# Queries, keys and values laid out ahead of the launch, instead of transposed on the chip, in attention with two dense layers

## The chip, the cores and the metric

One core of one Trainium2 chip. A time is the device time of one execution of the whole program in microseconds (us). Engines: TensorE (PE for matmuls, PEld for its weight loads), VectorE (DVE), ScalarE (ACT), GpSimd (POOL) and SyncE (SP), which only issues transfers. SPq and ACTq are the queues on which SP and ScalarE issue transfers.

## The reference

Attention with 4 batches, 8 heads, 576 positions and head dimension 64, and then two layers over 2304 tokens:

```python
scores = scale * np.matmul(q, k.transpose(0, 1, 3, 2))
cum = np.cumsum(np.maximum(s, 0.0), axis=-1)
bias = -(cum[:, :, :, None] - cum[:, :, None, :])
scores = np.where(causal, -1e9, scores + np.minimum(bias, 0.0))
attn = softmax(scores)                       # with 1e-9 added to the sum
x = (attn @ v).transpose(0, 2, 1, 3).reshape(2304, 512)
x = leaky_relu(x @ w_in, 0.01) @ w_out       # 512 -> 2048 -> 512
out = softplus(x @ w2_in) @ w2_out           # 512 -> 2048 -> 512
```

Everything is 32-bit. The matmuls of the layers run as three products of a high and a low part.

## The kernel before

The program has an attention stage and a main stage. The attention stage goes over 16 pairs of heads (`p`, from 0 to 15, four pairs to a batch). The 576 positions are four blocks of 128 and a tail of 64. Each pair is worked off in four units, in the order: block 3, the tails of both heads together, block 2, blocks 1 and 0. The loop at L454 is a pipeline by hand: step `n` = 4`p` + `i` issues the scores of unit `n`+1, masking, maxima (L316) and exponentials (L330) of unit `n`, the division (L341) of unit `n`−1, the transposes of the probabilities (L353, L358) of unit `n`−2, and the evacuation (L370, L372) of unit `n`−3. `pv` (L374) multiplies by the values at `i` = 0 and 2, for the pair before. All engines work in the order of the program; `later(n, fn)` and `tick()` put a piece of work some half-steps further on.

Scores need queries and keys with the head dimension on partitions: tiles `Q` (128 x 640) and `K` (128 x 576), where the two heads of a pair lie in partitions 0 to 63 and 64 to 127. The queries of the two tails stand in columns of their own, with zeros in the other head's partitions. The decay bias comes as two rows for each operand, `BQ` and `BK`, added by a second matmul into the same bank. All of these have two buffers, by the parity of `p`. The bias rows are made once (`decay`, L152), written to a scratch tensor `bb_d` and read back pair by pair (`rows`, L227); for pair 0 they are moved straight from the tile `bb`.

Queries and keys arrive in HBM as batch, head, position, dimension. `load` (L210) brings them into staging tiles `rawq`, `rawk` (one buffer each) and `rawl` (the tails of both), two transfers for each with rows of 256 bytes. `prep` (L241) transposes them on TensorE: four transposes for `q`, four for `k`, one for the tails, into the single PSUM bank "a", which `pv` uses as well. Half a step later ScalarE copies the queries into `Q` (L256), VectorE copies the keys (L258) and the three pieces of the tails (L260, L263). `prep` of pair `p`+1 happens at `i` = 0 (queries), 1 (keys) and 2 (tails); right behind it stands the load for pair `p`+2. At `i` = 0 the bias rows of pair `p`+1 follow on SP's queue. Values of pair `p`+1 are loaded at `i` = 3 by three transfers (L221 twice, L225).

Beside this runs a filler (`Fill`, L499). `step` loads and splits weights of the first layer at fixed steps up to 45, and `run` issues one filler unit of twelve matmuls for each step (L141 or L586), once the tokens of a whole batch are done and the weights are there. So the first pairs have no filler, and later ones one unit in every step; what is left is worked off at the end. After the attention stage, the main stage runs the remaining groups of both layers with an order of its own (the loop at L732).

Of the kernel before, what the change touches and what calls it, by code (L numbers as in the profile page):

```python
# [9 lines left out]
F32 = mybir.dt.float32  # L10
# [3 lines left out]
AF = mybir.ActivationFunctionType  # L14
# [3 lines left out]
P = 128  # L18
# [11 lines left out]
@with_exitstack  # L30
def attn_moe_moe(ctx, tc, q, k, v, s, w1i, w1o, w2i, w2o, out):
    nc = tc.nc
    B, H, S, D = q.shape
    NT, DM = out.shape
    DFF = w1i.shape[1]
    KD = DM // P
# [3 lines left out]
    NP = B * NPAIR  # L40
    NB = S // P
    TL = S - NB * P
# [5 lines left out]
    def pool(name, bufs=1, **kw):  # L48
        return tc.tile_pool(name=name, bufs=bufs, **kw)
# [14 lines left out]
    def later(n, fn, *args):  # L64
        todo.setdefault(clock[0] + n, []).append((fn, args))

    def tick():
        clock[0] += 1
        for fn, args in todo.pop(clock[0], ()):
            fn(*args)  # L70
# [5 lines left out]
    def move(dst, src, queue=nc.sync):  # L76
        queue.dma_start(dst.bitcast(F32), src.bitcast(F32))
# [74 lines left out]
    def decay(cp, first):  # L152

        BH = B * H
        c0 = cp.tile([BH, S], F32, tag="c0", name="c0")
        c1 = cp.tile([BH, S], F32, tag="c1", name="c1")
        bb = cp.tile([BH, 2, 2, S], F32R, tag="bb", name="bb")
        one = bb[:, 0, 0, :].bitcast(F32)
        nc.sync.dma_start(c0, s.rearrange("b h s -> (b h) s"))
        first()  # L160
        nc.vector.memset(one, 1.0)

        nc.vector.tensor_scalar(c0, c0, 0.0, 1.0 / scale, op0=ALU.max, op1=ALU.mult)
        nc.vector.tensor_tensor_scan(c1, one, c0, 0.0, op0=ALU.mult, op1=ALU.add)
        nc.scalar.activation(bb[:, 1, 0, :], c1, AF.Copy)
        nc.scalar.activation(bb[:, 0, 0, :], c1, AF.Copy, scale=-1.0)
        hi = bb[:, 1, 0, :].bitcast(F32)
        nc.vector.tensor_tensor(bb[:, 1, 1, :], c1, hi, op=ALU.subtract)
        nc.vector.tensor_tensor(bb[:, 0, 1, :], hi, c1, op=ALU.subtract)
        return bb  # L170


    def attention(att, ps, fills):
        ident = att.tile([P, P], F32, tag="ident", name="ident")
# [7 lines left out]
        Q, K = two("Q", [P, ZQ]), two("K", [P, S])  # L182
        BQ, BK = two("BQ", [P, ZQ], F32R), two("BK", [P, S], F32R)
        V = two("V", [P, NB + 1, 2, D])
        raw = {nm: att.tile([P, NB, 2, D], F32, tag="raw" + nm, name="raw" + nm) for nm in "qk"}
        raw["l"] = att.tile([P, 2, D], F32, tag="rawl", name="rawl")

        PA = att.tile([P, 2, NB, P + TL], F32, tag="PA", name="PA")
        PZ = att.tile([P, 2, TL], F32, tag="PZ", name="PZ")
# [1 line left out]
        def blank(i):  # L191
            bq, bk = BQ[i].bitcast(F32), BK[i].bitcast(F32)
            nc.gpsimd.memset(bq, 0.0)
            nc.gpsimd.memset(bk, 0.0)
            for j in range(2):
                for c in own[j]:
                    nc.gpsimd.memset(bq[j * D:j * D + 2, c], 1.0)
                nc.gpsimd.memset(bk[j * D + 32:j * D + 34], 1.0)
                nc.gpsimd.memset(Q[i][(1 - j) * D:(2 - j) * D, NB * P + j * TL:NB * P + (j + 1) * TL], 0.0)

        def zeros():
            for i in range(2):
                nc.gpsimd.memset(V[i][TL:, NB, :, :], 0.0)
            nc.gpsimd.memset(PZ[TL:], 0.0)

        def heads(p):
            b, hp = divmod(p, NPAIR)
            return b, slice(2 * hp, 2 * hp + 2)

        def load(p, nm):  # L210
            if p >= NP:
                return
            b, hs = heads(p)
            src = {"q": q, "k": k, "v": v}.get(nm)
            if nm == "l":
                for x, r in ((q, slice(0, TL)), (k, slice(TL, 2 * TL))):
                    nc.sync.dma_start(raw["l"][r], x[b, hs, NB * P:, :].rearrange("h p d -> p h d"))
                return
            t = V[p % 2] if nm == "v" else raw[nm]
            for j in range(2):  # L220
                nc.sync.dma_start(  # L221
                    t[:, :NB, j, :], src[b, hs.start + j, :NB * P, :].rearrange("(c p) d -> p c d", p=P)
                )
            if nm == "v":
                nc.sync.dma_start(t[:TL, NB, :, :], src[b, hs, NB * P:, :].rearrange("h p d -> p h d"))  # L225

        def rows(p, src, queue=(nc.sync, nc.sync)):  # L227

            if p < NP:
                b, hs = heads(p)  # L230
                for j in range(2):
                    h, r = b * H + hs.start + j, j * D
                    of = lambda e, c: src[h, e, :, c] if src is bb_d else src[h:h + 1, e, :, c]
                    n = 0
                    for c in own[j]:
                        m = n + c.stop - c.start
                        move(BQ[p % 2][r + 32:r + 34, c], of(0, slice(n, m)), queue[j])
                        n = m
                    move(BK[p % 2][r:r + 2], of(1, slice(0, S)), queue[j])

        def prep(p, nm):  # L241

            if p >= NP:
                return
            tag, bufs = ("a", 1) if p or nm == "q" else ("m", 1) if nm == "k" else ("t", 2)
            pm = ps.tile([P, 512], F32, tag=tag, name="pt_qk", bufs=bufs)
            if nm == "l":
                nc.tensor.transpose(pm[:, :P], raw[nm].rearrange("p h d -> p (h d)"), ident)
            else:
                for c in range(NB):  # L250
                    nc.tensor.transpose(pm[:, c * P:(c + 1) * P], raw[nm][:, c].rearrange("p h d -> p (h d)"), ident)  # L251

            def out():
                qt, kt = Q[p % 2], K[p % 2]
                if nm == "q" or nm == "k" and not p:
                    nc.scalar.activation((qt if nm == "q" else kt)[:, :NB * P], pm, AF.Copy)  # L256
                elif nm == "k":
                    nc.vector.tensor_copy(kt[:, :NB * P], pm)  # L258
                else:
                    nc.vector.tensor_copy(kt[:, NB * P:], pm[:, TL:2 * TL])  # L260
                    for j in range(2):
                        r = slice(j * D, (j + 1) * D)
                        nc.vector.tensor_copy(qt[r, NB * P + j * TL:NB * P + (j + 1) * TL], pm[r, :TL])  # L263

            later(1, out)


        class Unit:
# [152 lines left out]
                )  # L421

        def first():
            for nm in "qkl":
                load(0, nm)

        with pool("cum", side="right") as cp:
            bb = decay(cp, first)
            blank(0)
            for nm in "qkl":  # L430
                prep(0, nm)
                tick()
            tick()
            rows(0, bb, (nc.sync, nc.scalar))
            masks()
            zeros()
            blank(1)
            load(1, "q")
            load(0, "v")
            move(bb_d, bb)  # L440
            load(1, "k")
            load(1, "l")
        fill = fills()
        order = [[NB - 1], [], [NB - 2], [1, 0]]
        units = [(p, ts) for p in range(NP) for ts in order]
# [8 lines left out]
        for n in range(len(units) + 3):  # L454
            p, i = divmod(n, len(order))
            u0, u1, u2, u3 = (live.get(n - d) for d in range(4))
            start(n + 1)
            if u0:
                u0.maxima(0)
                u0.exps(0)  # L460
            if u1:
                u1.divisors()
                u1.norm(0)
            if u2:
                u2.transpose(0)
            if u3:
                u3.evacuate(1)
            if i == 0:
                prep(p + 1, "q")
                load(p + 2, "q")  # L470
                rows(p + 1, bb_d)
            elif i == 2:
                prep(p + 1, "l")
                load(p + 2, "l")
            tick()
            if n == len(units):
                fill.free = [("m", 1), ("s0", 2), ("s1", 2)]
            fill.step(n)
            if u0:
                u0.maxima(1)  # L480
                u0.exps(1)
            if u1:
                u1.norm(1)
            if u2:
                u2.evacuate(0)
                u2.transpose(1)
            if i == 1:
                prep(p + 1, "k")
                load(p + 2, "k")
            elif i == 3 and p + 1 < NP:  # L490
                load(p + 1, "v")
            elif i in (0, 2) and p:
                pv(p - 1, i == 0)
            if n >= len(units):
                fill.run()
            tick()
# [224 lines left out]
    for gi, (layer, g) in enumerate(groups[1:]):  # L721
        a, z = start[groups[gi]], start[layer, g]
        when = [a + 2, a + 5, a + 8, a + 11, z - 3, z, z - 1, z + 2]
        for j, n in enumerate(when):
            if gi == 0 and j < 4:
                continue
            f, nm = divmod(j, 2)
# [4 lines left out]
    for n, (layer, g, c, is_first, is_last, f) in enumerate(steps):  # L732
        N = c[1]
        cols = slice(c[0], c[0] + N)
        ps = ps_h.tile([P, 512], F32, tag="h", name="ps_h")
# [14 lines left out]
_OUT = ((2304, 512), "float32")  # L750


# [18 lines left out]
```

## Time and profile before

| what | us |
|---|---|
| median of 3 runs (lowest, highest) | 1041.98 (1041.75, 1042.41) |
| the profiled execution | 1041.97 |
| its span | 1040.2 |

| engine | busy us | share of the span |
|---|---|---|
| TensorE matmuls | 1009.9 | 97% |
| TensorE weight loads | 829.6 | 80% |
| VectorE | 512.5 | 49% |
| ScalarE | 545.1 | 52% |
| GpSimd | 581.3 | 56% |

The span is what lies between the first and the last instruction of the profiled execution. Busy times of different engines overlap. A busy TensorE isn't one at its peak: matmuls are pipelined, and the record of one is longer than the time by which it delays the next. The chain of work that ended last is followed back from the last instruction; a piece of it is the time by which that piece moved the end, and "issue" in it is time in which an engine waited for nothing that the profile shows.

### The profile page before, as it was taken

How to read it: one execution, taken by the hardware profiler on the slowest of the kernel's cores; microseconds unless marked ns; L12 is line 12 of the kernel's file. 1: busy time of each engine (PE TensorE's matmuls, PEld its weight loads, DVE VectorE, ACT ScalarE, POOL GpSimd, SP SyncE). 2: the span in 40 equal slices, each digit the busy share in tenths (PEclk: the TensorE clock that was granted, in tenths of full speed). 3: DMA queues.
4: the chain of work that ended last, by engine and by line, in shares of the span. 5: the costliest groups of instructions: out<-in, count | busy, mean ns of one | idle time of the engine just before them, and what ended most of it. 6: DMA issues, size and time to landing. Idle time of an engine off the chain costs nothing.

```text
span 1040.2 us, 15671 instructions
## 1 busy us (share of the span) xinstructions
PE 1009.9 (97%) x5632; PEld 829.6 (80%) x5632; DVE 512.5 (49%) x1174; ACT 545.1 (52%) x1170; POOL 581.3 (56%) x592
## 2 busy tenths in 40 slices
PE   7899999999999999999999998999999999999998
PEld 4668788888898888888888886888777887788886
DVE  5886756555202222222232245645675677567443
ACT  4776767665436333333344354676556545564452
POOL 5765544543327433643456667666866676667453
PEclk9999999999999999999999999999999999999999
DMA  6433433231053101210121021001200121010202
GB/s 146 126 86 79 106 89 99 73 77 37 24 183 119 41 1 41 81 41 1 49 74 41 1 80 42 25 17 41 81 27 15 41 82 37 5 40 21 82 21 81
DMA packets 89070, 61.20 MB, mean 59 GB/s; under 512 B 59616, under 2 KB 82656, under 8 KB 88960
## 3 DMA queue, kind: packets, MB, share of 16 engines
q1 hardware_dynamic: 88980, 60.18, 19.6%
q8 instruction: 45, 0.74, 0.3%
q14 instruction: 33, 0.27, 0.1%
q10 hardware_dynamic: 12, 0.01, 0.0%
HBM read 51.60 MB, written 8.55 MB: 58 GB/s over the span
## 4 chain that ended last, share of the span: by engine, by line
PE 71%; POOL 10%; DVE 8%; issue 6%; ACT 4%; DVEq 0%; POOLq 0%; ACTq 0%
PE ps_h L141 29%; PE ps_out L698 26%; PE ps_o L586 4%; PE pt_v L389 4%; PE pt_s L297 3%; POOL t L666 3%; PE pt_t L358 3%; POOL gl L148 2%; POOL wm L118 2%; DVE wm L112 2%; PE pt_s L287 2%; ACT sc L330 1%; DVE wm L115 1%; DVE wm L109 1%; PE pt_qk L251 1%
## 5 line engine op out<-in xcount | busy, mean ns | idle before, releaser
L148 POOL TENSOR_TENSOR gl<-gf,gh 128x512 fp32r<-128x512 f32 (+2 forms) x148 | 177.8, 1202 | 238.3 <-ACT gh L147 230.9
L141 PE MATMUL ps_h<-xh,wih 128*128 128x512 f32 (+2 forms) x688 | 247.5, 360 | 1.0 <-ACT o L590 0.5
L141 PE MATMUL ps_h<-xl,wih 128*128 128x512 f32 (+2 forms) x688 | 245.6, 357 | 0.0
L141 PE MATMUL ps_h<-xh,wil 128*128 128x512 f32 (+2 forms) x688 | 244.5, 355 | 0.0
L341 POOL TENSOR_SCALAR sc<-sc,st 128x512 f32<-128x512 f32 (+4 forms) x160 | 87.7, 559 | 121.3 <-DVE st L337 38.9
L141 PEld LDWEIGHTS ps_h<-xh,wih 128*128 128x128 f32 x688 | 130.0, 189 | 21.6 <-ACT o L590 0.8
L141 PEld LDWEIGHTS ps_h<-xl,wih 128*128 128x128 f32 x688 | 130.0, 189 | 19.1
L141 PEld LDWEIGHTS ps_h<-xh,wil 128*128 128x128 f32 x688 | 129.9, 189 | 18.6
L709 DVE TENSOR_TENSOR acc<-ps_out,acc 128x512 f32<-128x512 f32 (+1 forms) x114 | 67.7, 655 | 128.0 <-PE ps_out L698 128.0
L147 ACT ACTIVATE gh<-gf 128x512 fp32r<-128x512 f32 (+2 forms) x148 | 85.3, 576 | 85.0 <-DVE gf L671 84.1
L652 ACT ACTIVATE gf<-ps_h 128x512 f32<-128x512 f32 (+2 forms) x68 | 36.6, 538 | 171.8 <-PE ps_h L141 171.8
L671 DVE TENSOR_TENSOR gf<-gf,t 128x512 f32<-128x512 f32 (+1 forms) x80 | 56.0, 700 | 133.6 <-POOL t L666 133.6
L109 DVE TENSOR_SCALAR wm<-wm 128x512 f32<-128x512 f32 x64 | 42.6, 666 | 156.3 <-ACT wm L103 147.7
L698 PE MATMUL ps_out<-woh,gh 128*128 128x512 f32 x288 | 115.1, 400 | 3.0 <-DVE acc L709 2.0
L698 PE MATMUL ps_out<-wol,gh 128*128 128x512 f32 x288 | 114.2, 397 | 0.0
L330 ACT ACTIVATE sc<-sc,st 128x512 f32<-128x512 f32 (+2 forms) x144 | 83.5, 582 | 56.9 <-DVE st L316 23.4
L118 POOL TENSOR_TENSOR wm<-wm,wt 128x512 int32<-128x512 int32 x64 | 88.0, 1376 | 28.2 <-DVE wm L115 28.2
L666 POOL TENSOR_TENSOR t<-e,t 128x512 f32<-128x512 f32 (+1 forms) x80 | 98.1, 1226 | 0.0
L698 PE MATMUL ps_out<-gh,woh 128*128 128x512 f32 (+2 forms) x272 | 97.1, 366 | 0.0
L698 PE MATMUL ps_out<-gh,wol 128*128 128x512 f32 (+2 forms) x272 | 96.8, 364 | 0.0
L698 PE MATMUL ps_out<-woh,gl 128*128 128x512 f32 x288 | 81.6, 401 | 5.5 <-POOL gl L148 5.5
L316 DVE CUSTOM_DVE_ANT_0 sc<-pt_s,mask 128x512 f32<-128x512 f32 (+2 forms) x144 | 66.5, 481 | 38.1 <-PE pt_t L358 24.2
(105 smaller groups left out, 1815.0 us busy)
## 6 DMA issues: line engine op xcount, KB each, us to landing
rawi<-in_moe_w_in SPq DMA_DIRECT2D x32, 512.0 KB
rawo<-in_moe_w_out SPq DMA_DIRECT2D x32, 512.0 KB
out<-acc SPq DMA_DIRECT2D x18, 256.0 KB
rawq<-in_q SPq DMA_DIRECT2D x32, 128.0 KB
rawk<-in_k SPq DMA_DIRECT2D x32, 128.0 KB
V<-in_v SPq DMA_DIRECT2D x32, 128.0 KB
part<-o SPq DMA_DIRECT2D x24, 144.0 KB
acc<-part SPq DMA_DIRECT2D x6, 576.0 KB
```

The source lines that it names most:

```text
L109: nc.vector.tensor_scalar(mf, mf, D_MIN, D_MAX, op0=ALU.max, op1=ALU.min)
L118: nc.gpsimd.tensor_tensor(m, m, t, op=ALU.add)
L141: nc.tensor.matmul(ps, a, b, start=n == 0, stop=n == 3 * KD - 1)
L147: nc.scalar.activation(gh, gf, AF.Copy)
L148: nc.gpsimd.tensor_tensor(gl, gf, gh.bitcast(F32), op=ALU.subtract)
L316: nc.vector.tensor_tensor_reduce(out=self.sc[:, j, c], in0=self.ps[j][:, c], in1=m, scale=-scale, scalar=3.0e38, op0=ALU.add, op1=ALU.min, ...
L330: nc.scalar.activation(x, x, AF.Exp, scale=-1.0, bias=self.stat(0, e), accum_out=self.stat(1, e))
L341: nc.gpsimd.tensor_scalar(x, x, self.stat(2, e), 1.0, op0=ALU.mult, op1=ALU.mult)
L666: nc.gpsimd.tensor_tensor(t, e, t, op=ALU.subtract)
L671: nc.vector.tensor_tensor(gf, gf, t, op=ALU.add)
L698: nc.tensor.matmul(ps, a, b, start=f == 0 and m == 0, stop=f == G - 1 and m == 2)
L709: nc.vector.tensor_tensor(d, o, d, op=ALU.add)
```

## The change

Queries, keys and values get another layout in HBM, made by `lay_out` ahead of the launch, outside the time measured. For each pair, `q` is a block of 128 x 640 and `k` one of 128 x 576, both with the head dimension on partitions and `q` with its zeros for the tails in it; `v` is a block of 128 x 5 x 2 x 64, padded with zeros behind the tail. `load` becomes one transfer for each tensor and pair, straight into `Q`, `K` or `V`. `prep`, its transposes and copies, and the staging tiles are gone, with the memsets of `Q` and `V`. In the loop, the loads of `q` and `k` for pair `p`+1 now stand together at `i` = 0, ahead of the bias rows. For pair 0, the keys come over ScalarE's queue.

```diff
-        raw = {nm: att.tile([P, NB, 2, D], F32, tag="raw" + nm, name="raw" + nm) for nm in "qk"}
-        raw["l"] = att.tile([P, 2, D], F32, tag="rawl", name="rawl")
...
-                nc.gpsimd.memset(Q[i][(1 - j) * D:(2 - j) * D, NB * P + j * TL:NB * P + (j + 1) * TL], 0.0)
...
-            for i in range(2):
-                nc.gpsimd.memset(V[i][TL:, NB, :, :], 0.0)
             nc.gpsimd.memset(PZ[TL:], 0.0)
...
-        def load(p, nm):
...
+        def load(p, nm, queue=nc.sync):
+            if p < NP:
+                t, x = {"q": (Q, q), "k": (K, k), "v": (V, v)}[nm]
+                queue.dma_start(t[p % 2], x[p])
...
-        def prep(p, nm):
...
         def first():
-            for nm in "qkl":
-                load(0, nm)
+            load(0, "q")
+            load(0, "k", nc.scalar)
...
             blank(0)
-            for nm in "qkl":
-                prep(0, nm)
-                tick()
             tick()
             rows(0, bb, (nc.sync, nc.scalar))
             masks()
             zeros()
             blank(1)
-            load(1, "q")
             load(0, "v")
             move(bb_d, bb)
-            load(1, "k")
-            load(1, "l")
...
             if i == 0:
-                prep(p + 1, "q")
-                load(p + 2, "q")
+                load(p + 1, "q")
+                load(p + 1, "k")
                 rows(p + 1, bb_d)
-            elif i == 2:
-                prep(p + 1, "l")
-                load(p + 2, "l")
...
-            if i == 1:
-                prep(p + 1, "k")
-                load(p + 2, "k")
-            elif i == 3 and p + 1 < NP:
+            if i == 3 and p + 1 < NP:
                 load(p + 1, "v")
...
+def lay_out(name, a):
+    if name not in ("q", "k", "v"):
+        return np.ascontiguousarray(a)
+    B, H, S, D = a.shape
+    n, tl = S // P, S % P
+    a = a.reshape(B * H // 2, 2, S, D)
+    if name == "v":
+        r = np.zeros((B * H // 2, P, n + 1, 2, D), a.dtype)
+        r[:, :, :n] = a[:, :, :n * P].reshape(-1, 2, n, P, D).transpose(0, 3, 2, 1, 4)
+        r[:, :tl, n] = a[:, :, n * P:].transpose(0, 2, 1, 3)
+        return r
+    r = np.zeros((B * H // 2, 2, D, S + (tl if name == "q" else 0)), a.dtype)
+    r[..., :S] = a.transpose(0, 1, 3, 2)
+    if name == "q":
+        r[:, 1, :, S:] = r[:, 1, :, n * P:S]
+        r[:, 1, :, n * P:S] = 0
+    return r.reshape(-1, 2 * D, r.shape[-1])
```

## Rows read from the trace of the kernel before

**Rows 1.** The page, its first section: busy us of each engine, share of the span, instructions.

```profile
PE 1009.9 (97%) x5632; PEld 829.6 (80%) x5632; DVE 512.5 (49%) x1174; ACT 545.1 (52%) x1170; POOL 581.3 (56%) x592
```

**Rows 2.** Busy time of each engine in two stretches of the attention stage: the stretch, its length, busy us of the engines (instructions), the granted clock of TensorE (1.00 is full), the busy share of the transfer engines, and what they moved.

```profile
core 0: us, PE busy (x) PEld busy (x) DVE busy (x) ACT busy (x) POOL busy (x), PEclk, DMA share, GB/s
22.00:82.00 60.00, 54.20 (x430) 39.46 (x429) 51.25 (x187) 46.65 (x130) 37.34 (x53) 1.00 0.46 115
...
129.00:252.00 123.00, 122.56 (x1002) 102.36 (x1001) 71.56 (x279) 79.12 (x222) 54.82 (x88) 1.00 0.30 78
```

**Rows 3.** The chain of work that ended last, from 129 to 252 us, summed by engine and line as shares of that stretch.

```profile
by line: PE ps_o L586 19.5%; PE pt_v L389 17.2%; PE pt_s L297 17.1%; PE ps_h L141 14.3%; PE pt_t L358 13.5%; PE pt_s L287 6.4%; PE pt_qk L251 4.6%; PE pt_t L353 2.9%; PE pt_t L349 0.8%; ACT sc L330 0.7%; DVE K L258 0.6%; PE pt_qk L248 0.5%; 
```

**Rows 4.** The same chain over one pair of the dense stretch, from 182.3 to 200.4 us: the sums by line, and one of its 21 pieces (start us, length us, what).

```profile
by line: PE ps_h L141 35.0%; PE pt_s L297 18.5%; PE pt_v L389 16.7%; PE pt_t L358 13.7%; PE pt_s L287 6.9%; PE pt_qk L251 4.8%; PE pt_t L353 3.2%; PE pt_qk L248 0.6%; PE pt_t L349 0.6%
...
189.18 0.44 PE pt_qk L251 x4
```

**Rows 5.** The same chain over three pairs of the loose stretch, from 26.5 to 40, from 54.4 to 68 and from 100.7 to 113.9 us: those pieces that belong to the preparation of queries and keys (start us, length us, what).

```profile
31.29 0.60 DVE K L258
...
33.52 0.20 DVE K L260
33.72 0.12 DVE Q L263
...
33.86 0.05 DVE Q L263
...
39.56 0.45 PE pt_qk L251 x4
...
61.04 0.12 PE pt_qk L248
...
61.18 0.23 DVE K L260
61.41 0.12 DVE Q L263
...
61.55 0.24 DVE Q L263
...
100.68 0.60 ACT Q L256
...
107.24 0.12 PE pt_qk L248
...
107.39 0.22 DVE K L260
107.61 0.12 DVE Q L263
...
107.75 0.23 DVE Q L263
...
113.45 0.45 PE pt_qk L251 x4
```

**Rows 6.** The instructions on the tile `pt_qk`: line, engine, operation, how many, duration in ns (least/median/most), first and last start in us, shapes.

```profile
L251 PE MATMUL pt_qk<-ident,rawq x64: 272/273/447, 4.8 to 235.1; 128*128 128x128 f32 x64
...
L263 DVE COPY Q<-pt_qk x32: 202/217/229, 7.3 to 244.9; 64x64 f32<-64x64 f32 x32
L256 ACT ACTIVATE Q<-pt_qk x16: 576/597/599, 5.9 to 235.4; 128x512 f32<-128x512 f32 x16
...
L260 DVE COPY K<-pt_qk x16: 204/215/226, 7.2 to 244.6; 128x64 f32<-128x64 f32 x16
L258 DVE COPY K<-pt_qk x15: 677/692/693, 18.6 to 242.8; 128x512 f32<-128x512 f32 x15
```

**Rows 7.** Who waited for whom from 12.5 to 129 us: us in total, times, longest.

```profile
PEld pt_v L389 <- ACT Q L256: 2.7, 6, 0.6
...
PE pt_v L389 <- DVE Q L263: 1.1, 4, 0.4
```

**Rows 8.** The start in order of time, ScalarE's queue and TensorE (start us, length us, engine, line, operation, operands, how many, idle time before and what ended it).

```profile
7.16 2.01 ACTq L77 DMA_DIRECT2D BQ<-bb  x2
9.27 0.58 ACTq L77 DMA_DIRECT2D BK<-bb  x1
...
11.76 0.76 PE L297 MATMUL pt_s<-BK,BQ 64*128 64x512 f32 x1 [1.24 <-POOL Q L199]
```

**Rows 9.** SP's queue and TensorE in order of time, around one step of the loose stretch and one of the dense stretch: the last transfer of a value load, the first query load of the next step, and the first scores of the pair after it.

```profile
50.48 0.61 SPq L225 DMA_DIRECT2D V<-in_v  x1
54.20 0.92 SPq L221 DMA_DIRECT2D rawq<-in_q  x2
...
63.37 1.13 PE L297 MATMUL pt_s<-K,Q 64*128 64x512 f32 x4
...
177.75 0.61 SPq L225 DMA_DIRECT2D V<-in_v  x1
182.33 2.19 SPq L221 DMA_DIRECT2D rawq<-in_q  x2
...
194.73 1.13 PE L297 MATMUL pt_s<-K,Q 64*128 64x512 f32 x4
```

**Rows 10.** The columns of rows 2 for one microsecond at the start.

```profile
10.00:11.00 1.00, 0.53 (x1) 0.02 (x1) 0.31 (x1) 0.00 (x0) 0.91 (x5) 1.00 0.95 216
```

More of the change, by code (lines that the diff above doesn't have):

```diff
@@ L32, in attn_moe_moe @@
     nc = tc.nc
-    B, H, S, D = q.shape
+    B, H, S = s.shape
+    D = v.shape[-1]
     NT, DM = out.shape
@@ L208, in heads @@
             return b, slice(2 * hp, 2 * hp + 2)
-        def load(p, nm):
[L211 to L225, printed above, removed]
+        def load(p, nm, queue=nc.sync):
+            if p < NP:
+                t, x = {"q": (Q, q), "k": (K, k), "v": (V, v)}[nm]
+                queue.dma_start(t[p % 2], x[p])
         def rows(p, src, queue=(nc.sync, nc.sync)):
@@ L239, in rows @@
                     move(BK[p % 2][r:r + 2], of(1, slice(0, S)), queue[j])
-        def prep(p, nm):
[L243 to L265, printed above, removed]
         class Unit:
@@ L750 @@
 _OUT = ((2304, 512), "float32")
+def lay_out(name, a):
+    import numpy as np
+    if name not in ("q", "k", "v"):
[14 more added lines that the diff above has]
+    return r.reshape(-1, 2 * D, r.shape[-1])
 def kernel(**inputs):
@@ L760 @@
     for name in _INS:
-        a = np.ascontiguousarray(inputs[name])
+        a = lay_out(name, np.asarray(inputs[name]))
         if a.dtype == np.float64:
```

## The prediction

> **What bounds the kernel now.** I read the page first: 1040.2 us of span with TensorE busy 1009.9 of it [rows 1]. The profiled run took 1041.97 us, so 1.8 us lie around the span, and the median of the three runs is 1041.98: I can subtract from the profiled run directly. Then I read busy times by stretch, because the change touches only the attention stage. That stage has two regimes. From 22 to 82 us (almost no filler matmuls) nobody is full: in 60 us TensorE has 54.2 busy, VectorE 51.3, ScalarE 46.7. From 129 to 252 us, where one filler unit of twelve matmuls stands in every step, TensorE has 122.6 of 123.0 us [rows 2]. I call them the loose and the dense stretch.
>
> A busy share doesn't say what sets the end, so the third view is the chain of work that ended last. Over the dense stretch [rows 3] nearly all of it is TensorE lines; the parts that the change deletes are 4.6% (transposes of queries and keys, L251), 0.5% (of their tails, L248) and 0.6% (VectorE's copy of the keys, L258). Within one dense pair the chain is TensorE alone, with no wait and no issue gap, and four of those transposes hold it for 0.44 us [rows 4], 0.11 us each, although the record of one lasts 0.27 us [rows 6]: they overlap. In a loose pair the chain alternates between VectorE, ScalarE and TensorE, and the same preparation shows up in pieces of all three [rows 5].
>
> **What is deleted, and its price.** Per pair of heads: nine transposes on TensorE; on ScalarE one 0.60 us copy of Q; on VectorE copies of 0.69, 0.22 and two of 0.22 us [rows 6], 1.34 us in all. None of that is replaced on an engine; only transfers remain.
>
> Dense stretch: the deleted lines hold 4.6 + 0.5 + 0.6 = 5.7% of 123.0 us [rows 3] = 7.0 us. I take all of it. VectorE and ScalarE stand at 71.6 and 79.1 of 123.0 us there [rows 2], so no engine is near to replacing TensorE; the filler units and the remaining transposes (of the probabilities) are untouched and simply close up.
>
> Loose stretch, pairs 0 to 7: three of these eight pairs are shown. Their pieces of preparation add up to 0.60 + 0.20 + 0.12 + 0.05 + 0.45 = 1.42, to 0.12 + 0.23 + 0.12 + 0.24 = 0.71, and to 0.60 + 0.12 + 0.22 + 0.12 + 0.23 + 0.45 = 1.74 us [rows 5], mean 1.29; times eight, 10.3 us. Taking work off a chain can't give back more than the work's length on it, and gives less where a second chain is close behind. The ends are therefore 0 and 10.3. With three engines between 78% and 90% busy a second chain is close, but each of the three loses work too (1.34 us of VectorE, 0.60 of ScalarE, nine slots of 0.11 = 1.0 of TensorE per pair), so that chain shortens as well. I choose four fifths: 8.2 us.
>
> One deleted wait belongs here. The transposes' bank "a" in PSUM is single and shared with the value matmuls, which waited in the loose stretch 2.7 us for ScalarE's copy of Q and 1.1 us for VectorE's [rows 7]. Part of that is already in the pieces above; I add nothing for it, and keep 2.5 us, about two thirds of the two rows, for the upper end.
>
> The start: the first unit's bias matmul begins at 11.76 us, put down to a POOL memset. But that memset clears a buffer of the other parity; what it needs is the last bias row, which ScalarE's queue issues at 9.27 us for 0.58 us, behind two issues that take 2.01 us [rows 8]. So the end of the cumulative sums sets this moment, not the transposes before it, and deleting first transposes, four small Q memsets and two V memsets costs and gives nothing. What changes is that ScalarE's queue now issues the first key load well before the cumulative sums, and that two query issues and one value issue more no longer compete with the rows. The rows' issue could be quicker by up to 0.8 us (2.01 against twice 0.58 of the last issue [rows 8]), or everything could come later by the 0.58 us of one issue, if the key load gets in the way of the load of s. I take a gain of 0.3. TensorE's early matmuls are slow: the longest transpose took 447 ns against a median of 273 [rows 6], while the granted clock reads 1.00, its 2.4 GHz level, in both stretches shown [rows 2]. If the quick rate came later for want of transposes I could lose up to about 1 us of pair 0; before and after, TensorE is fed without a break from 11.76 us on, so I take 0.
>
> **What is moved.** The loads of Q and K for pair p+1 now write the operand tiles directly, and must wait for the scores of pair p−1 instead of for transposes; they stand on SP's queue ahead of five bias-row issues, the weight loads and the stores. Are they late? Today SP issues the last value load at 50.48 and the first query load of the next step at 54.20, because it waits for transposes; the pair that this load serves in the new scheme begins its scores at 63.37. In the dense stretch the three times are 177.75, 182.33 and 194.73 [rows 9]. The new load finds its buffer free when the value load has been issued, at about 51.1 and 178.4. Two issues of some 0.6 us, 128 x (640 + 576) x 4 bytes = 0.62 MB at the 216 GB/s of a busy microsecond [rows 10] = 2.9 us, and 1.9 us from the end of the last row's issue to its first use (9.85 to 11.76 [rows 8]): landed by about 57.1 and 184.4. That leaves 6 us and 10 us. The bias rows come some 1.7 us later and fit too; a 0.5 MB weight load in front would take 2.4 us and still fit. Cost nothing, and the cover is those 6 to 10 us. Fewer SP waits mean earlier weight loads, which nobody waits for.
>
> **Sum:** 1041.97 − 7.0 − 8.2 − 0.3 = 1026.5 us. Everything behind the attention stage should only shift.
>
> **Rivals.**
> (a) A second chain holds the loose pairs. If only a fifth of their 10.3 us comes back (2.1), the time is 1041.97 − 7.0 − 2.1 − 0.3 = 1032.6. For it: the loose chain is mixed, with ScalarE's exponentials and weight splits close by. Against: all three engines lose work.
> (b) TensorE doesn't bind the dense stretch, so that its 7.0 us are hidden: 1041.97 − 8.2 − 0.3 = 1033.5. For it: weight loads occupy only 102.4 of 123.0 us there [rows 2], so a sixth of TensorE could be slack. Against: the chain of a dense pair has no piece outside TensorE [rows 4]. The Trainium skill (Perfetto Trace Analysis, section Identifying the Most-Contended Engine) says that matmul occupancy is a poor measure of closeness to roofline and that LDWEIGHTS busy time should be used instead; by it the dense stretch would be 17% short of full, and this case would follow. The trace disagrees so far, since the chain shows back-to-back slots, which is a matter of order and not of peak.
> (c) More than the chain: all 10.3 us of the loose pairs, 2.5 of bank waits and 0.8 at the start give 1041.97 − 7.0 − 10.3 − 2.5 − 0.8 = 1021.4.
> (d) Slower: the new loads come late. Place: the first scores of each of pairs 1 to 15, which would wait for Q or K. It begins to count when the loads take 6 us (loose) to 10 us (dense) longer than worked out, and turns the sign when they take 15.5 / 15 = 1.0 us beyond that. At 2 us beyond, 15 x 2 = 30 us lost: 1041.97 − 15.5 + 30 = 1056. For it: Q and K lost their staging tile, a pair less of run-ahead. Against: the slack above, and rows of 2.5 KB in place of 256 bytes.
>
> **How the numbers follow.** Forecast 0.62, (a) 0.13, (b) 0.06, (c) 0.14, (d) 0.03, and 0.02 for a mixture that cancels. The predicted time is the forecast's, 1026.5. The range reaches from a little below (c), 1020, to a little above (b), 1034: it holds the first four cases with some room for their ends left outside. A measurement can tell 0.2% (2.1 us) from no change here; (a), (b), (c) and the forecast are all faster by more. Faster 0.95, same 0.02, slower 0.03.
>
> **What would show it.** Right: lines L251, L248 and the copies gone; a dense pair shorter by 1.0 us, still TensorE from end to end; loose pairs about 1.0 us shorter; the first bias matmul still near 11.5 us; everything behind the attention stage shifted whole. Wrong: scores waiting for a transfer into Q, K or BQ (d); dense pairs of unchanged length with new idle time on TensorE (b); loose pairs of unchanged length, with ScalarE or VectorE taking the place of the deleted pieces on the chain (a).

## The result, and the profile after

The changed kernel takes 1026.22 us (median of 4 runs, 1025.72 to 1026.45) against 1042.2 for the kernel before on the same chip: ratio 0.9846, 95% interval 0.9829 to 0.9863. That is 16.0 us less; 15.5 were forecast, and the time lies in the range. In the profiled executions the span fell from 1040.2 to 1024.5 us.

The page of the changed kernel, its first section, answers to [rows 1]. TensorE lost 18.3 us of busy time, VectorE 14.4, ScalarE 7.3; GpSimd is about where it was.

```profile
PE 991.6 (97%) x5488; PEld 812.6 (79%) x5488; DVE 498.1 (49%) x1111; ACT 537.8 (52%) x1153; POOL 582.5 (57%) x586
```

The dense stretch has become shorter and starts earlier. Its busy times, and the chain that ended last summed over it (both of the changed kernel, 118 to 235 us), answer to [rows 2, 3].

```profile
118.00:235.00 117.00, 116.93 (x949) 96.74 (x948) 66.15 (x257) 77.03 (x217) 55.89 (x89) 1.00 0.29 92
...
by line: PE ps_o L533 20.3%; PE pt_s L256 18.9%; PE pt_v L348 18.1%; PE ps_h L143 15.0%; PE pt_t L317 14.9%; PE pt_s L246 7.4%; PE pt_t L312 3.0%; PE pt_t L308 0.8%; ACT sc L289 0.7%; ACT PA L329 0.4%; ACT xh L355 0.4%; issue 0.1%
```

Nothing took the place of the deleted lines: TensorE still has 116.9 of 117.0 us, and its other lines moved together. The chain over one dense pair of the changed kernel (167.97 to 185.08 us) shows the same as [rows 4], without the transposes of queries and keys:

```profile
by line: PE ps_h L143 37.8%; PE pt_s L256 19.5%; PE pt_v L348 17.6%; PE pt_t L317 14.5%; PE pt_s L246 7.2%; PE pt_t L312 3.4%; PE pt_t L308 0.6%
```

A pair's length can be read off the matmuls: it is the distance between the first score matmul on the two tails (128x288, L287 before, L246 after) in one pair and in the next. I use that for every kernel below. Lengths in us, worked out from those start times in each trace:

| kernel | first tail matmul at | pairs 0 to 7 | pairs 8 to 14 | a dense pair (11) |
|---|---|---|---|---|
| before | 12.46 | 114.32 | 124.61 | 18.09 |
| changed | 13.40 | 104.67 | 117.18 | 17.11 |
| transposes only | 12.86 | 107.82 | 124.05 | 18.09 |
| transposes, ScalarE copy | 12.87 | 109.99 | 124.05 | 18.09 |
| transposes, VectorE copies | 13.14 | 112.18 | 124.58 | 18.09 |
| transposes, both copies | 13.31 | 114.75 | 124.58 | 18.09 |
| copies only, from SBUF | 13.07 | 111.54 | 117.19 | 17.12 |
| Q and K two steps later | 13.28 | 106.07 | 117.19 | 17.12 |
| values in 256-byte rows | 12.33 | 105.16 | 117.22 | 17.12 |
| keys of pair 0 over SP | 12.45 | 104.16 | 117.19 | 17.12 |

So the change gave 7.43 us in the dense pairs and 9.65 in pairs 0 to 7, and cost 0.94 at the start. Behind pair 14 another 0.44 us were lost (0.25 in a second profile of the same kernel, below); that leaves the 15.7 us of the spans. Pair 5 counts among pairs 0 to 7 but is a dense one: 18.09 us before, 17.11 after.

At the start, what was scored first is now ready sooner, but its bias rows are not. In order of time on all engines of the changed kernel, beside [rows 8]:

```profile
0.73 0.40 SPq L161 DMA_DIRECT2D c<-in_s  x1
0.76 0.42 ACTq L210 DMA_DIRECT2D K<-in_k  x1
...
2.96 0.57 POOL L198 MEMSET BK<- 2x576 f32 x1
3.02 0.81 DVE L165 TENSOR_SCALAR c<-c 32x576 f32<-32x576 f32 x1 [1.57 <-DMA c<-in_s]
...
3.87 1.35 DVE L166 TENSOR_TENSOR_SCAN c<-bb,c 32x576 f32<-32x576 f32 x1
...
7.54 1.79 ACTq L79 DMA_DIRECT2D BQ<-bb  x2
9.37 0.56 ACTq L79 DMA_DIRECT2D BK<-bb  x1
...
12.70 0.76 PE L256 MATMUL pt_s<-BK,BQ 64*128 64x512 f32 x1 [1.71 <-DMA BK<-bb]
```

ScalarE's queue begins to issue the first key load 0.03 us after SP's queue begins to issue the load of s. The cumulative sum starts at 3.87 us; before, it started at 3.33 (all engines, the kernel before):

```profile
2.85 0.45 DVE L163 TENSOR_SCALAR c<-c 32x576 f32<-32x576 f32 x1 [1.41 <-DMA c<-in_s]
2.95 0.87 POOL L198 MEMSET BK<- 2x576 f32 x1
...
3.33 1.34 DVE L164 TENSOR_TENSOR_SCAN c<-bb,c 32x576 f32<-32x576 f32 x1
```

VectorE's first operation on s began 0.10 us ahead of GpSimd's memset before, and took 0.45 us; now it begins 0.06 us behind that memset and takes 0.81.

### The profile page after: what moved, and what is told of

It is laid out like the page before. It is cut to its first block, busy times and chain, and to the rows that moved or that the text cites. A ratio compares the mean times of both kernels' runs of the same rounds, so it can differ in the third digit from the quotient of the medians.

```text
span 1024.5 us, 15084 instructions
## 1 busy us (share of the span) xinstructions
PE 991.6 (97%) x5488; PEld 812.6 (79%) x5488; DVE 498.1 (49%) x1111; ACT 537.8 (52%) x1153; POOL 582.5 (57%) x586
## 4 chain that ended last, share of the span: by engine, by line
PE 76%; POOL 8%; DVE 6%; issue 5%; ACT 3%; DMA 1%; SPq 0%; ACTq 0%; DVEq 0%; POOLq 0%
PE ps_h L143 31%; PE ps_out L645 29%; PE pt_v L348 4%; PE ps_o L533 4%; PE pt_s L256 3%; PE pt_t L317 3%; POOL t L613 2%; POOL gl L150 2%; POOL wm L120 2%; PE pt_s L246 1%; DVE wm L114 1%; ACT sc L289 1%; DVE wm L111 1%; POOL wil L130 1%; DVE sc L275 1%
```

## The experiments

**Put the transposes back, alone.** For pairs 1 to 15, at their old places, of a constant tile (`ident`), into the bank "a"; nobody reads them.

```diff
+        def prep(p, nm):
+            if p >= NP:
+                return
+            pm = ps.tile([P, 512], F32, tag="a", name="pt_qk", bufs=1)
+            for c in range(1 if nm == "l" else NB):
+                nc.tensor.transpose(pm[:, c * P:(c + 1) * P], ident, ident)
```

> The changed kernel, with nine transposes per pair put back on TensorE at their old places (steps i = 0, 1, 2, for pairs 1 to 15, into bank "a"), but of a constant tile and with nobody reading them: no copies, no staging loads. Theory (the gain is the work taken off the chain): each dense pair is 9 x 0.11 = 1.0 us longer again, 17.1 to 18.1, so +7 over seven dense pairs, and the loose pairs get back the transposes' own chain pieces, about 0.4 us each, so +3: near 1036. Rival (TensorE has slack in the dense stretch, LDWEIGHTS fill only five sixths of it): dense pairs stay at 17.1, time 1026 to 1029. Rival (the gain came from the transfers, fewer and with larger rows): 1026.

Measured: 1035.48 us, ratio to before 0.9938 (95% interval 0.9922 to 0.9955; below in brackets), near the 1036 expected. The dense pair is back at 18.09 us and pairs 8 to 14 are 6.87 us longer than in the changed kernel, seven times 0.98. The chain over such a pair (174.1 to 192.2 us, this kernel) has the transposes in it again, L232, and still nothing but TensorE:

```profile
by line: PE ps_h L143 35.0%; PE pt_s L264 18.4%; PE pt_v L356 16.7%; PE pt_t L325 13.7%; PE pt_s L254 8.2%; PE pt_qk L232 5.4%; PE pt_t L320 3.2%; PE pt_t L316 0.6%
```

Rival (b) falls with it: the dense stretch pays for every slot, though weight loads fill only 96.7 of 117.0 us. The rival on transfers falls too. In pairs 0 to 7 the transposes alone cost 3.15 us, close to the 3 expected, but not by 0.4 in each pair as I had reasoned: 1.51 fall in pair 0 and 1.00 in the dense pair 5, while pairs 2 to 4 don't notice them (12.79, 13.52 and 14.11 us against 12.82, 13.51 and 14.07).

**Put transposes and copies back.** The same with ScalarE's and VectorE's copies half a step later, into a tile `junk` that nobody reads.

```diff
+            def out():
+                if nm == "q":
+                    nc.scalar.activation(junk[:, 0], pm, AF.Copy)
+                elif nm == "k":
+                    nc.vector.tensor_copy(junk[:, 1], pm)
+                else:
...
+            later(1, out)
```

> The changed kernel, with transposes and copies both put back as dummies: nine transposes of a constant tile per pair into bank "a", then ScalarE's copy of 128x512 and VectorE's copies of 128x512, 128x64 and twice 64x64 out of it into a tile that nobody reads. The loads stay as changed (one large transfer each, into the operand tiles). Theory: the whole gain of pairs 1 to 15 is gone: dense pairs 18.1, loose pairs as before, 1041 to 1043. Rival (transfers, SP's waits, run-ahead): no more than 1030.

Measured: 1042.48 us, 1.0007 [0.9998, 1.0016]. The whole gain is gone, with all the new transfers in place; pairs 1 to 7 have their old lengths to 0.03 us, and only pair 0 is longer than it was (12.00 against 11.59). So layout and transfers give nothing by themselves: what counts is the work that they make unnecessary.

**Put the copies back, alone,** out of a constant tile in SBUF, by `tensor_scalar` on VectorE.

```diff
+            def two_ops(o, x):
+                nc.vector.tensor_scalar(o, x, 1.0, 0.0, op0=ALU.mult, op1=ALU.add)
+            def out():
+                if nm == "q":
+                    nc.scalar.activation(junk[:, 0], mask, AF.Copy)
+                elif nm == "k":
+                    two_ops(junk[:, 1], mask)
...
```

> The changed kernel, with the copies alone put back as dummies: per pair one ScalarE copy of 128x512 (0.6 us) and VectorE operations of 128x512 (0.67 us), 128x64 and twice 64x64, from a constant tile in SBUF into a tile that nobody reads. No transposes. Theory: dense pairs stay at 17.1 (VectorE and ScalarE have a third to two fifths of that stretch free), loose pairs get back the copies' chain pieces, 0.6 to 0.9 us each for seven of them: +4 to +6, 1030 to 1032. Rival (the gain in loose pairs is TensorE's): 1026 to 1028.

Measured: 1032.48 us, 0.9911 [0.9896, 0.9925]. Dense pairs: unchanged, as expected, 117.19 us. Loose pairs: 6.9 us longer, more than expected. But these stand-ins are not the copies they stand for, as their durations show (busy us, mean ns of one, idle us before; the copies out of PSUM are those of [rows 6]):

```profile
L233 DVE TENSOR_SCALAR junk<-mask 64x64 f32<-64x64 f32 x30 | 13.2, 441 | 0.2
L233 DVE TENSOR_SCALAR junk<-mask 128x512 f32<-128x512 f32 x15 | 7.4, 495 | 0.0
L233 DVE TENSOR_SCALAR junk<-mask 128x64 f32<-128x64 f32 x15 | 6.1, 408 | 0.0
```

The 128x512 ones average 495 ns against a median of 692 out of PSUM, but the 64x64 ones 441 against 217, so that VectorE's four take 1.79 us in a pair and not 1.34. So the run settles the dense pairs, not the size in the loose ones; the next two use true copies.

**Transposes with the copies of one engine.** The kernel with both, less one branch of `out`.

```diff
-                if nm == "q":
-                    nc.scalar.activation(junk[:, 0], pm, AF.Copy)
```

> Nine dummy transposes per pair as in dummy_transposes (1035.5), and with them VectorE's copies out of that bank (128x512, 128x64, twice 64x64) into a tile that nobody reads; no copy on ScalarE. Theory (the chain pieces of the loose pairs add up by engine): VectorE's pieces average 0.7 us in the three pairs shown, seven pairs, +5: 1040 to 1041, dense pairs unchanged at 18.1. Rival (it is ScalarE's copy, and the wait of the value matmuls for it, that matters in loose pairs): 1036.

```diff
-                elif nm == "k":
-                    nc.vector.tensor_copy(junk[:, 1], pm)
-                else:
...
```

> Nine dummy transposes per pair as in dummy_transposes (1035.5), and with them ScalarE's copy out of that bank alone; no copies on VectorE. Theory: ScalarE's pieces average 0.2 us in the three pairs shown, seven pairs, +1.4: 1037, dense pairs unchanged. Rival: 1041. If this run and the one with VectorE's copies add up to clearly less than the 7.0 us between dummy_transposes and dummy_prep, the loose pairs are held by either of two chains, and the pieces don't add.

Measured: 1040.68 us with VectorE's copies, 0.9988 [0.9978, 0.9998]; 1038.34 with ScalarE's, 0.9964 [0.9951, 0.9977]. Over pairs 0 to 7, VectorE's copies add 4.36 us to the transposes, ScalarE's 2.17, and both together 6.93: they nearly add, with 0.4 us that appear only when both are there. VectorE is the larger part, as the chain had it. ScalarE's copy costs more than expected (2.2 us against 1.4), and the waits of this last kernel from 12 to 129 us point to a place (us in all, times, longest):

```profile
PEld pt_v L369 <- ACT junk L237: 2.8, 6, 0.6
PE pt_v L369 <- ACT junk L237: 1.4, 4, 0.4
```

The value matmuls wait for the copy to leave bank "a", as in [rows 7]. No run has the copy without this wait, so its share isn't shown.

**Load Q and K two steps later.** Bias rows stay where they were.

```diff
             if i == 0:
-                load(p + 1, "q")
-                load(p + 1, "k")
                 rows(p + 1, bb_d)
+            elif i == 2:
+                load(p + 1, "q")
+                load(p + 1, "k")
```

> The changed kernel, with the loads of Q and K for the next pair issued two steps later (i = 2 in place of i = 0; the bias rows stay at i = 0). Theory by my slack numbers (landed about 6 us after the earliest issue, first scores 6 us later in loose pairs, 10 us later in dense ones): two steps take 7 us in loose pairs and 8.6 us in dense ones, so the loose pairs wait about 1 us each (7 x 1 = 7) and the dense ones just not: 1030 to 1036. If the loads have much less slack than I worked out: 3 us for each of 15 pairs, over 1065. If they are covered altogether: 1026.

Measured: 1026.82 us, 0.9856 [0.9841, 0.9871]: the "covered altogether" case, and not the 1030 to 1036 of my slack numbers, but for 1.7 us in pair 0. There the key load of pair 1 is issued at 15.64 us, beside weight and value loads, and the chain of this kernel holds it for 6.22 us; TensorE stands 2.07 us idle for it. A piece of that chain, and TensorE in order of time:

```profile
15.64 6.22 DMA K<-in_k
...
21.99 1.09 PE L256 MATMUL pt_s<-K,Q 64*128 64x512 f32 x3 [2.07 <-DMA K<-in_k]
```

In pairs 2 to 5 the loads moved by little: SP isn't tied to the steps and issues as soon as its own waits allow. For pair 4 it issues at 49.33 us for scores at 60.34, a lead of 11.0 us, against 12.5 in the changed kernel. In the dense pairs they did move, down to a lead of 4.4 to 4.5 us in four of them. SP's queue and TensorE, this kernel:

```profile
161.31 0.42 SPq L210 DMA_DIRECT2D Q<-in_q  x1
161.79 0.44 SPq L210 DMA_DIRECT2D K<-in_k  x1
...
165.78 1.13 PE L256 MATMUL pt_s<-K,Q 64*128 64x512 f32 x4
```

The queries' issue begins 4.5 us before the first scores that need them, and no time is lost: pairs 8 to 14 take 117.19 us. The changed kernel issues its loads far ahead, for instance 12.5 us before the scores in a loose pair and 16.6 in a dense one (SP's queue and TensorE, in two stretches):

```profile
46.50 0.69 SPq L210 DMA_DIRECT2D Q<-in_q  x1
...
59.01 1.13 PE L256 MATMUL pt_s<-K,Q 64*128 64x512 f32 x4
...
164.99 0.42 SPq L210 DMA_DIRECT2D Q<-in_q  x1
...
181.58 1.13 PE L256 MATMUL pt_s<-K,Q 64*128 64x512 f32 x4
```

**Values in three transfers with rows of 256 bytes.** From the new layout.

```diff
+                if nm == "v":
+                    for j in range(2):
+                        queue.dma_start(t[p % 2][:, :NB, j, :], x[p][:, :NB, j, :])
+                    queue.dma_start(t[p % 2][:, NB], x[p][:, NB])
+                    return
```

> The changed kernel, with the values of each pair brought in by three transfers again, two of them in rows of 256 bytes. Theory (transfers are hidden): no change, 1025 to 1027. Rival (larger rows give part of the gain): up to a third of it back, 1028 to 1031.

Measured: 1025.51 us (1024.43 to 1025.74). No price in the time, and none from pair 1 on. In pair 0 the value load does reach the chain, and that pair takes 9.41 us against 8.92 (8.53 in the second profile of the changed kernel). A piece of the chain of this run:

```profile
16.95 5.18 DMA V<-in_v
```

**The start.** The changed kernel once more, and three variants beside it on one chip.

> The changed kernel once more, beside the three variants of its start: 1026.2 within 0.5.

> The changed kernel, with the first key load on SP's queue behind the first query load, and not on ScalarE's. Theory A (the key load on the second queue runs beside the load of s and makes the cumulative sums 0.5 us late): first operation on s back from 3.02 to about 2.85, sums done 0.5 us earlier, and all with them: 1025.7. Theory B (what is late is only the landing of the last bias rows, because the value and query loads that follow compete with them): no change, 1026.2.

> The changed kernel, with the value load of pair 0 moved behind the bias rows of pair 1, and those rows put ahead of the Q and K loads of pair 1, so that only the copy of the bias rows into the scratch tensor runs beside the bias rows of pair 0. Theory B: the last bias row of pair 0 lands 1.9 us after its issue as in the kernel before, not 2.8: first bias matmul of the second head at 11.8 and not 12.7, 1025.3. Theory A: no change of that, 1026.2.

> Both start variants together. If A and B both hold: the first bias matmul of the second head at about 11.3, 1024.8. If one alone holds, as that one alone.

The edit of the second, that of the third, and both in the fourth:

```diff
-            load(0, "k", nc.scalar)
+            load(0, "k")
```

```diff
-            load(0, "v")
             move(bb_d, bb)
...
             if i == 0:
+                if not p:
+                    rows(1, bb_d)
                 load(p + 1, "q")
                 load(p + 1, "k")
-                rows(p + 1, bb_d)
+                if p:
+                    rows(p + 1, bb_d)
+                else:
+                    load(0, "v")
```

Measured: 1025.36 (1025.09 to 1026.23), 1024.98 (1024.48 to 1025.71), 1025.28 (1025.04 to 1026.07) and 1025.01 us (1024.59 to 1025.06). The first, the changed kernel again, is 0.9 us below the 1026.22 of its first measurement, more than the 0.5 allowed for; the times of all four overlap, so the traces decide. With the keys of pair 0 on SP's queue the cumulative sum starts at 3.24 us, and in the fourth kernel at 3.28; with them on ScalarE's queue at 3.87, 3.87 and 3.86. So the sum is late because of where the key load is issued, as theory A has it. Keys over SP, all engines in order of time:

```profile
2.71 0.50 DVE L165 TENSOR_SCALAR c<-c 32x576 f32<-32x576 f32 x1 [1.26 <-DMA c<-in_s]
...
2.95 0.78 POOL L198 MEMSET BK<- 2x576 f32 x1
...
3.24 1.35 DVE L166 TENSOR_TENSOR_SCAN c<-bb,c 32x576 f32<-32x576 f32 x1
...
8.77 0.56 ACTq L79 DMA_DIRECT2D BK<-bb  x1
...
11.76 0.76 PE L256 MATMUL pt_s<-BK,BQ 64*128 64x512 f32 x1 [1.35 <-DMA BK<-bb]
```

How late it is, GpSimd's memset seems to decide. Of the thirteen profiles here, the ten with the keys on ScalarE's queue have the first operation on s begin anywhere from 2.97 to 3.35 us, always behind the memset, and end at 3.83 each time. In the other three it begins before 2.95, ends by 3.30, and the memset takes 0.78 to 0.87 us and not 0.57. No run moves the memset, so this is read from the times alone and not shown by experiment.

Theory B isn't borne out: the later landing of the last bias row in the first profile (first use at 12.70) didn't come again in the second profile of the same kernel (12.26), and the quiet start had 12.27. The ten profiles with the keys on ScalarE's queue range from 11.64 (the values in 256-byte rows) to 12.70; why they differ is not shown. The Trainium skill (DMA: Bandwidth & Descriptors, section Issuing engines are not separate DMA queues) says that transfers started by different engines share the same transfer engines, and that only issue time is saved. Here it agrees: with the keys on the second queue the first scores began at 4.60 us in place of 4.93, which moved nothing behind them, and the load of s came late. Keys over SP is the fastest version measured, 0.9840 [0.9826, 0.9853], but by less than the runs of either scatter.

## Why the prediction was right

**Dense stretch:** 7.0 forecast, 7.43 measured. The step was read from the chain, and the transposes put back alone take 6.87 of it away again. Nearly all of the rest is pair 9 (17.10 us before, 15.61 after, 16.57 with transposes alone, 17.10 with VectorE's copies too), where VectorE's copy of the keys stood on the chain of the kernel before:

```profile
154.49 0.69 DVE K L258
```

**Loose stretch:** 8.2 forecast as four fifths of 10.3; 9.65 measured. The mechanism was right, and the factor a guess that was too low. Read over all eight pairs, with the bounds of the table, the deleted pieces on the chain of the kernel before add up to 9.9 us: 3.8 of TensorE, 4.9 of VectorE, 1.2 of ScalarE. Nearly all of it came back, so no discount was called for. That three pairs gave a fair mean (1.29 against 1.24) was luck, since the pairs differ. Pair 0 holds 2.01 us, because transposes are still slow there (0.85 us for four, against 0.44 in [rows 4]). Its pieces, from the chain of the kernel before:

```profile
15.22 0.85 PE pt_qk L251 x4
...
17.31 0.59 PE pt_qk L251 x4
...
19.97 0.12 PE pt_qk L248
...
20.12 0.23 DVE K L260
20.34 0.12 DVE Q L263
...
20.48 0.10 DVE Q L263
```

Pair by pair the pieces hold only roughly: pair 0 gave 2.67 us for its 2.01, pair 6 1.67 for 1.29, pair 1 0.76 for 0.97, and pair 3 nothing for 0.71 (13.51 both times). In pair 3 a second chain was ready, as rival (a) had it for all: from 48.16 to 61.67 us the chain of the changed kernel has no TensorE in it. What I set at nothing, the wait for bank "a", may be part of what ScalarE's copy costs (2.2 us against 1.2 on the chain).

**Start:** the step with the wrong sign. The quicker issue for which I took 0.3 us came: ScalarE's queue needs 2.39 us for its rows (7.54 to 9.93) and not 2.69 (7.16 to 9.85 [rows 8]). But the sum ahead of the rows starts 0.54 us late. That is near the 0.58 that I gave the other end, yet not for its reason, one issue's time: what came late is the landing of s. And from the end of its issue to its first use the last row took 2.77 us (2.34 in the second profile) in place of 1.91. All in all the bias matmul came 0.94 us later (0.50 in the second profile), and the sign that I had named, a bias matmul still near 11.5 us, was not borne out: it came at 12.70. Keys over SP bring the sum back, but the last row still takes 2.43 us (9.33 to 11.76); why is not shown.

TensorE's quick rate, for which I took nothing, came later too, though the granted clock reads 1.00 from 16 to 18 us in both kernels. The same four score matmuls of pair 0, before and after (TensorE in order of time):

```profile
16.01 1.13 PE L297 MATMUL pt_s<-K,Q 64*128 64x384 f32 x4
...
16.09 1.65 PE L256 MATMUL pt_s<-K,Q 64*128 64x384 f32 x4
```

TensorE did not work without a break from 11.76 us on as I had assumed for both, but from 12.70. Whether the slower matmuls cost anything beyond the late start is not shown.

**Moved loads:** cost nothing, as forecast. In the dense pairs the landing time in the working (about 6 us from the first issue) was too long: 4.5 us are enough, and rival (d) was further off than I said. In pair 0, beside weight and value loads, it was not too long: there the keys took 6.2 us when they were loaded late. That nobody waits for the earlier weight loads held only in part: in the first profile the chain of the changed kernel goes through one,

```profile
21.45 3.22 DMA rawi<-in_moe_w_in
```

in the second it doesn't, and what that costs isn't shown.

The total came out within 0.5 us by luck as well: the loose pairs gave 1.4 us more than forecast and the dense ones 0.4, while the start took 1.2 us that were forecast otherwise and the part behind pair 14 another 0.4.

## What to carry to other kernels

Work that an engine does only to turn data round is priced by its slot on the chain, not by its record: in the dense pairs a transpose of 0.27 us was worth 0.11. Where the chain was one engine from end to end, deleting that engine's work returned all of it, and other engines' work put back by itself cost nothing. Where the chain alternates, add its pieces up over all pairs and put each part back by itself: the sum came within 0.3 us here, single pairs missed by up to 0.7. A load with slack is best kept off the moment at which a small one decides the start.

## What the runs showed that I had not expected

VectorE's small operations out of SBUF were slower on average than those out of PSUM: 64x64 took 441 ns against 217. By themselves they are quicker; 16 of the 30 took 175 to 192 ns. The slow ones stand beside GpSimd: each of the six longest, 1.17 to 1.19 us, began 0.2 us behind a GpSimd operation of 1.3 us and ended within 0.06 us of its end. One of them, in the kernel with the copies alone:

```profile
45.82 1.30 POOL L120 TENSOR_TENSOR wm<-wm,wt 128x512 int32<-128x512 int32 x1
46.01 1.17 DVE L233 TENSOR_SCALAR junk<-mask 64x64 f32<-64x64 f32 x1
```

The Trainium skill (SBUF — State Buffer, section Who interferes with whom) says that copies and `tensor_scalar` can take a port pair that VectorE shares with GpSimd, and that then one of the two is held up for a whole instruction. These ends fit that, and so does the memset at the start; no run here takes GpSimd away.
